# Attention and two mixture layers in fp32 on one core: two score slots per head for the first eight head pairs, and an instruction order planned with other durations

## The chip, the cores and the metric

One core of one Trainium2 chip runs the whole program. The metric is device time in microseconds of one execution, shown as the median of several runs.

## The reference

The kernel must compute, in fp32 accuracy, a thresholded attention (4 batches, 8 heads, 576 positions, 64 wide), a dense gated layer on its output (2304 tokens, 512 to 2048 to 512), and a layer of 8 experts of which each token takes one:

```python
scores = scale * q @ k.T                          # per batch and head, 576 x 576
scores = where(scores >= max(scores) - tau, scores, -1e9)
attn   = exp(scores - max(scores)); attn /= attn.sum() + 1e-9
x      = (attn @ v) -> 2304 x 512
h = x @ w_in; x = (h * sigmoid(h)) @ w_out        # the dense layer, 2048 wide
e = argmax(normalised x @ normalised expert_emb)  # one of 8 experts per token
out = gate * relu(x @ w1[e]) @ w2[e]              # 1024 wide
```

The weights of the dense layer come as fp64 and are decoded to fp32 on the chip.

## The kernel before

**The work.** Heads go in 16 pairs. A pair takes nine steps: four chunks of 128 query rows for each of its two heads (ch 0 to 3, h 0 and 1), and a ninth in which the last 64 rows of both heads stand together (ch 4). For each step TensorE (PE) writes 576 score columns to PSUM (`score_pe`, L490), VectorE (DVE) takes the row maximum (L496), ScalarE (ACT) makes the threshold (L499) and the exponential (L501), and DVE masks and sums (L516), so that P stands in SBUF. PE then transposes P (L553, L561, L569, L573), ACT or DVE copies the transposes out (L278, L280), and PE multiplies them with v (`values`, L645) in two parts per pair. The two heads of a chunk lie in the upper and lower 64 rows of the PE array and their score matmuls run side by side; in P v the two heads lie side by side in the columns. So PE works with three divisions of its array: by rows for scores, by columns for P v, whole or nearly whole for the rest. The denominators (L598 to L624) are transposed by one matmul of PE per pair (L603), go to DRAM and back, and multiply the pair's output, which then goes to DRAM.

**Filler.** The dense layer's first six of sixteen column tiles are computed inside the attention, for the blocks of 256 tokens whose batches are complete (`moe_block`, six blocks of nine): products with w_in (L685, 72 matmuls a block) and with w_out (L719, 36 a block). They have the lowest rank: PE does them when nothing of the attention can start. Decoding of the dense weights runs on DVE (L321, L326), ACT (L313, L314) and GpSimd (POOL, L331 to L335, L391) in the first part. After the attention come the rest of the dense layer (`products`, L1084, and the second product behind it) and the experts.

**PSUM.** All eight banks of 512 fp32 columns are one tile, `banks`. `BANKS` names the slots: score slots of two banks each (S0 at bank 0, S1 at 2, S2 at 6, the third only for the first `WIDE` = 40 of the 144 steps), one bank T for transposes, and M for everything else: bank 5 at first, more once the score slots that hold them are given up (`more_banks`).

**The order.** No engine chooses at run time: every engine has a fixed list, in order. `Plan` makes it while the program is built. Each `plan.task` names an engine, a duration in us that the author wrote down, the tasks it comes after, the slots (`Token`) it takes and gives, a rank, and for some a second engine that may do it instead (`alt`). `Plan.run` always starts the task that can start first by these durations, and the rank decides near ties. The semaphores are put in afterwards, by the framework, from what the instructions read and write in that order; a bank of PSUM is the unit there.

Of the kernel before, what the change touches and what calls it, by code (L numbers as in the profile page):

```python
# [9 lines left out]
F32 = mybir.dt.float32  # L10
# [15 lines left out]
    "kr": 2, "qr": 2, "vs": 2, "m": 4, "e": 2, "P": 2, "Pm": 1, "l": 2,  # L26
# [63 lines left out]
class Task:  # L90
    def __init__(self, eng, us, fn, rank, take, give, slack, more, alt):
        self.eng, self.us, self.fn, self.rank, self.take, self.give = eng, us, fn, rank, take, give
        self.slack, self.more, self.alt, self.wait, self.after, self.next, self.end = slack, more, alt, 0, [], [], None


class Plan:


    def __init__(self, bufs, banks):
# [8 lines left out]
        self.kind, self.kinds = None, defaultdict(list)  # L108

    def task(self, eng, us, fn, after=(), take=(), give=(), rank=0.0, slack=0.0, more=0.0, alt=None):  # L110

        t = Task(eng, us, fn, rank, take, give, slack, more, alt)
# [44 lines left out]
    def start(self, t, eng):  # L157
# [9 lines left out]
        return at  # L167
# [36 lines left out]
    def run(self):  # L204
        while self.n:
# [19 lines left out]
            if eng == "pe":  # L225
                us = self.clock(a, us)
            self.free[eng] = a + us
# [16 lines left out]
class Kernel:  # L244
# [44 lines left out]
    def weight_piece(self, new, src, n, name):  # L289
# [43 lines left out]
        def large():  # L333
# [7 lines left out]
            ("dve", 0.55 if wide else 0.4, dve, ["wa"], []), ("dve", 0.7 if wide else 0.55, top, [], ["wraw"]),  # L341
            ("pool", 1.26 if wide else 0.76, pool, [], ["wr"]), ("pool", 2.4 if wide else 1.5, large, [], ["wm"]),
# [39 lines left out]
    def weight_plan(self, new):  # L382
# [3 lines left out]
        def keep(o, dst):  # L386
# [6 lines left out]
            return [("act", 0.6, act, [], []), ("pool", 1.26, sub, [], ["wa"], ("dve", 0.69))]  # L393
# [85 lines left out]
    def score_pe(self, st, ch, ws, uses):  # L479

        nc = self.nc
        for h, (w, use) in enumerate(zip(ws, uses)):
            w.nm = f"{ch}{h}" + st.nm
            w.S = self.banks[:, use.slot:use.slot + 2]
        lhsT = st.o.q[:, 128 * ch:128 * ch + 128]
        for a in range(2):
            for h, w in enumerate(ws):
# [3 lines left out]
                    w.S[:, a, :288], lhsT=lhsT[rows], rhs=st.o.k[rows, 288 * a:288 * a + 288], start=True, stop=True  # L491
                )

    def score_max(self, w):
        w.m = self.apool.tile([128, 2], F32, tag="m", bufs=4, name="m" + w.nm)
        self.nc.vector.tensor_reduce(out=w.m[:, 0:1], in_=w.S[:, :, :288], axis=AX.XY, op=ALU.max, negate=True)  # L496

    def score_exp(self, w):
        self.nc.scalar.activation(out=w.m[:, 1:2], in_=w.m[:, 0:1], func=AF.Identity, bias=self.ntau, scale=-1.0)  # L499
        w.e = self.apool.tile([128, 2, 288], F32, tag="e", bufs=2, name="e" + w.nm)  # L500
        self.nc.scalar.activation(out=w.e, in_=w.S[:, :, :288], func=AF.Exp, bias=w.m[:, 0:1])  # L501

    def score_mask(self, step, w):
# [4 lines left out]
        if ch < 4:  # L508
            if h == 0:
                st.P[ch] = self.apool.tile([128, 1152], F32, tag="P", bufs=2, name=f"P{ch}" + st.nm)  # L510
# [1535 lines left out]
```

## Time and profile before

| | |
|---|---|
| median of 3 runs | 1076.0 us (1073.23 to 1076.56) |
| the profiled execution | 1079.59 us, its span 1077.8 us |
| PE busy | 983.5 us (91%) |
| DVE, ACT, POOL busy | 727.1, 529.6, 436.6 us |
| mean granted TensorE clock | 0.966 |
| denominators of pair 8 of 16 on PE | at 228.75 us |
| denominators of pair 16 | at 454.35 us |

The profile's times count from the span's start. A matmul's record lasts longer than the time until the next one may start, so a busy PE is not a PE at its peak. An fp32 matmul of L490 or L645 gives two records. "Idle ... <-" behind a row says how long the engine did nothing before it and what ended that.

### The profile page before, as it was taken

Reading aid. Unit: us, or ns where it says so; the run is one execution under the profiler, and the core shown is the slowest. Engines: PE = TensorE matmul, PEld = TensorE weight load, DVE = VectorE, ACT = ScalarE, POOL = GpSimd, SP = SyncE. Lnnn points to the kernel's source line nnn. Section 1 sums busy time; section 2 is a strip of 40 time slices with the busy share of each in tenths; the row PEclk is TensorE's granted clock in tenths of the full one; section 3 lists DMA queues with packets and bytes.
Section 4 is the critical chain, followed back from the end, with each engine's and each line's share of the span. In section 5 each row is a group of like instructions: output and inputs, shape, how many; then the busy total and the mean of one; then the engine's idle time right before and its main releaser. Section 6 shows DMA issues by size and latency. Waiting matters only on the chain. (4 is left out here: it accounts for less than half of the span.)

```text
span 1077.8 us, 18270 instructions
## 1 busy us (share of the span) xinstructions
PE 983.5 (91%) x6379; PEld 804.6 (75%) x6379; DVE 727.1 (67%) x1693; ACT 529.6 (49%) x1262; POOL 436.6 (41%) x447
## 2 busy tenths in 40 slices
PE   3878789989998999988999999999897999999995
PEld 2545466766665667667878989899886999999994
DVE  5798876767676777567768888888766534545521
ACT  4688755545464556456653333333553443454510
POOL 4997841112021012049944444444424443333210
PEclk9799989999999999999999999999997999999998
DMA  4444632222222121164423211111537554555400
GB/s 155 133 149 155 213 103 77 77 71 83 64 76 81 61 72 48 57 207 138 162 94 129 83 37 57 60 61 40 161 116 228 159 165 152 169 168 179 138 32 15
DMA packets 76398, 119.27 MB, mean 111 GB/s; under 512 B 11668, under 2 KB 38596, under 8 KB 76305
## 3 DMA queue, kind: packets, MB, share of 16 engines
q1 hardware_dynamic: 71857, 107.68, 31.4%
q0 software_dynamic: 4448, 10.40, 3.1%
q8 instruction: 51, 0.84, 0.3%
q14 instruction: 42, 0.34, 0.1%
HBM read 94.04 MB, written 24.82 MB: 110 GB/s over the span
## 5 line engine op out<-in xcount | busy, mean ns | idle before, releaser
L496 DVE TENSOR_REDUCE m<-banks 128x1 f32<-128x576 f32 x144 | 103.1, 751 | 39.0 <-PE banks L490 38.1
L516 DVE SCALAR_TENSOR_TENSOR P<-banks,m,e 128x576 f32<-128x576 f32 x128 | 103.9, 815 | 34.1 <-ACT e L501 33.8
L1065 DVE TENSOR_TENSOR wle<-rawe,whe 128x512 fp32r<-128x512 f32 x95 | 69.0, 751 | 81.5 <-ACT whe L1061 80.9
L1061 ACT ACTIVATE whe<-rawe 128x512 fp32r<-128x512 f32 x128 | 77.0, 625 | 85.7 <-PE banks L1899 29.7
L278 ACT ACTIVATE p<-banks 128x512 f32<-128x512 f32 (+2 forms) x143 | 66.6, 478 | 102.0 <-PE banks L553 83.9
L553 PE MATMUL banks<-ident,P 128*128 128x128 f32 x512 | 86.7, 294 | 32.5 <-DVE P L516 26.9
L553 PEld LDWEIGHTS banks<-ident,P 128*128 128x128 f32 x512 | 58.8, 147 | 72.9 <-DVE P L516 27.4
L501 ACT ACTIVATE e<-banks,m 128x576 f32<-128x576 f32 x144 | 105.5, 733 | 1.3 <-DVE P L516 1.2
L645 PE MATMUL banks<-p,v 128*64 128x256 f32 (+3 forms) x640 | 99.2, 438 | 6.1 <-ACT p L278 4.8
L490 PE MATMUL banks<-k,q 64*128 64x288 f32 x540 | 101.6, 448 | 1.2 <-DVE P L516 1.2
L1304 ACT ACTIVATE t<-banks 128x256 f32<-128x256 f32 x108 | 41.1, 381 | 107.5 <-PE banks L1084 105.0
L1065 POOL TENSOR_TENSOR wle<-rawe,whe 128x512 fp32r<-128x512 f32 x33 | 42.6, 1293 | 99.5 <-ACT whe L1061 77.3
L645 PEld LDWEIGHTS banks<-p,v 128*64 128x64 f32 (+1 forms) x640 | 43.1, 143 | 49.1 <-issue 20.7
L490 PEld LDWEIGHTS banks<-k,q 64*128 64x128 f32 x540 | 57.7, 195 | 23.0 <-issue 10.6
L1309 DVE SCALAR_TENSOR_TENSOR g<-t,banks 128x256 f32<-128x256 f32 x108 | 45.1, 418 | 37.0 <-ACT t L1304 33.7
L1084 PE MATMUL banks<-xs_6h,wh 128*128 128x256 f32 x216 | 61.5, 285 | 0.0
L1084 PE MATMUL banks<-xs_6h,wl 128*128 128x256 f32 x216 | 61.0, 283 | 0.0
L1084 PE MATMUL banks<-xs_6l,wh 128*128 128x256 f32 x216 | 60.9, 282 | 0.0
L710 POOL TENSOR_TENSOR gl<-g,gh 128x256 fp32r<-128x256 f32 x25 | 18.2, 731 | 103.4 <-ACT gh L704 102.2
L621 POOL TENSOR_TENSOR t<-t,rb 128x576 f32<-128x576 f32 x14 | 19.9, 1420 | 91.1 <-ACT t L278 48.6
L280 DVE COPY p<-banks 128x512 f32<-128x512 f32 (+2 forms) x81 | 43.9, 545 | 16.2 <-PE banks L553 11.8
L499 ACT ACTIVATE m<-m,ntau 128x1 f32<-128x1 f32 x144 | 41.5, 288 | 14.0 <-DVE m L496 13.6
(574 smaller groups left out, 3137.1 us busy)
## 6 DMA issues: line engine op xcount, KB each, us to landing
rawe<-moe_w SPq DMA_DIRECT2D x64, 512.0 KB, 4.5
wraw<-moe_w_in SPq DMA_DIRECT2D x12, 512.0 KB, 3.7
wraw<-moe_w_out SPq DMA_DIRECT2D x10, 512.0 KB, 3.4
q<-q SPq DMA_DIRECT2D x15, 320.0 KB, 3.9
v<-v SPq DMA_DIRECT2D x16, 288.0 KB, 3.5
x_dram<-t SPq DMA_DIRECT2D x16, 288.0 KB, 2.8
part<-po SPq DMA_DIRECT2D x18, 256.0 KB, 3.0
xc<-x_dram SPq DMA_DIRECT2D x18, 256.0 KB, 3.2
```

Of the source, the lines that this page charges most:

```text
L278: self.nc.scalar.activation(out=out, in_=src, func=AF.Copy)
L280: self.on[on].tensor_copy(out=out, in_=src)
L490: nc.tensor.matmul(w.S[:, a, :288], lhsT=lhsT[rows], rhs=st.o.k[rows, 288 * a:288 * a + 288], start=True, stop=True)
L496: self.nc.vector.tensor_reduce(out=w.m[:, 0:1], in_=w.S[:, :, :288], axis=AX.XY, op=ALU.max, negate=True)
L501: self.nc.scalar.activation(out=w.e, in_=w.S[:, :, :288], func=AF.Exp, bias=w.m[:, 0:1])
L516: self.nc.vector.scalar_tensor_tensor(out=P.rearrange("p (a x) -> p a x", a=2), in0=w.S[:, :, :288], scalar=w.m[:, 1:2], in1=w.e, op0=ALU. ...
L553: nc.tensor.transpose(T[:, 128 * j:128 * j + 128], st.P[ch][:, c:c + 128], self.ident)
L645: nc.tensor.matmul(w.av[HALF[h], :nq], lhsT=st.o.vn[rows, k, :], rhs=st.pts[part][rows, k, :], start=(j == 0), stop=(j == 4),)
L1061: self.nc.scalar.activation(out=o.tiles[0][:, 2 * a:2 * a + 2], in_=o.raw[:, 2 * a:2 * a + 2], func=AF.Copy)
L1065: self.on[on].tensor_tensor(out=o.tiles[1][:, to], in0=o.raw[:, to], in1=o.tiles[0][:, to].bitcast(F32), op=ALU.subtract)
L1084: self.nc.tensor.matmul(h[:, :n], lhsT=lhs(a, kk), rhs=z[:, kk, :], start=(kk == 0 and i == 0), stop=(kk == 3 and i == 2))
L1309: nc.vector.scalar_tensor_tensor(out=o.g, in0=o.t, scalar=1.0, in1=self.banks[:, use.slot, :BLK], op0=ALU.add, op1=ALU.mult)
```

## The change

- **Score slots.** For the first 72 steps (eight pairs, before: 40 steps) each head has two slots of its own: A0 and A1 for h 0 in banks 0 to 2, B0 and B1 for h 1 in banks 3 to 5. A slot is 688 columns and holds the 576 scores as four pieces of 144 columns, 172 apart, so that no piece crosses a bank. Slot 0 lies in the first bank and in the first 148 columns of the second; slot 1 in the rest of the second and in the third. A score step pair is now 16 records of 144 columns there, where it was 8 of 288; after step 72 it is as before, with one slot per head. The exponentials have three buffers, before two.
- **M.** T is bank 6, M bank 7 alone until the last wide mask; then banks 2 and 5 come to M.
- **P v.** The five matmul pairs of a part are one task; they were five tasks.
- **Planner.** Each change between scores, P v and the rest costs 0.1 us in the plan (`SWITCH`), and many written durations are others.

The core of the diff:

```diff
-    "kr": 2, "qr": 2, "vs": 2, "m": 4, "e": 2, "P": 2, "Pm": 1, "l": 2,
+    "kr": 2, "qr": 2, "vs": 2, "m": 4, "e": 3, "P": 2, "Pm": 1, "l": 2,
-BANKS = {"S0": [0], "S1": [2], "S2": [6], "T": [4], "M": [5, 6, 7, 0, 1, 2, 3, 4]}
-WIDE = 40
+BANKS = {"A0": [0], "A1": [1], "B0": [0], "B1": [1], "T": [6], "M": [7, 2, 5, 0, 1, 3, 4, 6]}
+WIDE = 72
+PIECE, APART = 144, 172
+SWITCH = 0.1
...
-        return at
+        return at + SWITCH if eng == "pe" and t.mode != self.mode else at
...
-            w.S = self.banks[:, use.slot:use.slot + 2]
+            bank = 3 if use.tag[0] == "B" else 0
+            if use.wide:
+                at = 512 * bank + 4 * APART * use.slot
+                w.S = self.flat[:, at:at + 4 * APART].rearrange("p (a x) -> p a x", x=APART)[:, :, :PIECE]
+            else:
+                w.S = self.banks[:, bank:bank + 2, :288]
...
-                    w.S[:, a, :288], lhsT=lhsT[rows], rhs=st.o.k[rows, 288 * a:288 * a + 288], start=True, stop=True
+                    w.S[:, a], lhsT=lhsT[rows], rhs=st.o.k[rows, c * a:c * a + c], start=True, stop=True
...
-        self.more_banks = {bank: Token("gate") for bank in (0, 2, 4, 6)}
+        self.more_banks = {x: Token("gate") for x in ("wide", "narrow", "T")}
...
-                    turn = int(s + i) % (3 if s < WIDE else 2)
-                    w.use = Token(f"S{turn}")
+                    w.use = Token(f"{'AB'[i]}{(9 * n // 2 + n % 2 + (a + 1) // 2) % 2 if s < WIDE else 0}")
+                    w.use.wide = s < WIDE
...
-                    "pe", 0.97, partial(self.score_pe, st, ch, pe, [w.use for w in pe]), o.there + self.last_s,
+                    "pe", 1.18, partial(self.score_pe, st, ch, pe, [w.use for w in pe]),
+                    o.there + self.last_s + ([] if s < WIDE else self.last_wide),
...
-                "dve", 0.73, partial(self.score_mask, step, w), [t] + list(masks.values())[-1:],
+                "dve", 0.81, partial(self.score_mask, step, w), [t] + list(masks.values())[-1:],
...
-                for i, fn in enumerate(mms):
-                    t = plan.task(
-                        "pe", us, fn, (t,) if t else moved[part] + o.v_there + av[-1:],
+                t = plan.task(
+                    "pe", 5 * us, partial(run_all, mms), moved[part] + o.v_there + av[-1:],
+                    (tok,) if part else (tok, t_use), (part_use[part], o.v_use), rank=s + 1, mode="values",
+                )
```

What this does to the order, at three places. In the changed kernel L503 are the scores (L490 before), L567 and L575 transposes (L553, L561), L583 and L587 those of the last rows (L569, L573), L617 the denominators (L603), L659 P v (L645), L699 and L733 the dense layer's two products (L685, L719), L509 the maximum (L496), L530 the mask (L516), L515 the exponential (L501).

First, PE in the fourth pair (k_559 before, k_532 now): scores, transposes, P v and the denominators of the pair before it. Before:

```order
L490 MATMUL banks<-k_559,q_554 128x288 x4
L553 MATMUL banks<-ident,P_781 128x128 x4
L569 MATMUL banks<-ident,Pm 128x64 x4
L573 MATMUL banks<-ident,Pm 64x64
L569 MATMUL banks<-ident,Pm 128x64 x4
L573 MATMUL banks<-ident,Pm 128x64
L490 MATMUL banks<-k_559,q_554 128x288 x4
L603 MATMUL banks<-ident,l_629 9x128
L553 MATMUL banks<-ident,P_859 128x128 x4
L645 MATMUL banks<-p_763,v_452 64x320 x10
L553 MATMUL banks<-ident,P_859 128x128 x4
```

and now:

```order
L503 MATMUL banks<-k_532,q_513 128x144 x8
L567 MATMUL banks<-ident,P_779 128x128 x4
L617 MATMUL banks<-ident,l_645 9x128
L503 MATMUL banks<-k_532,q_513 128x144 x8
L583 MATMUL banks<-ident,Pm 128x64 x4
L587 MATMUL banks<-ident,Pm 64x64
L583 MATMUL banks<-ident,Pm 128x64 x4
L587 MATMUL banks<-ident,Pm 128x64
L567 MATMUL banks<-ident,P_891 128x128 x4
L659 MATMUL banks<-p_798,v_442 64x320 x10
L567 MATMUL banks<-ident,P_891 128x128 x4
```

The second chunk's scores moved ahead of the transposes of the last rows of the pair before, since a second slot of each head is there for them.

Second, what such instructions wait for, a little further in the same pair. DVE before (maxima of the third chunk of the third pair, both heads, a copy, and their masks):

```order
L496 TENSOR_REDUCE m2002_717<-banks_99 128x1 [waits PE_49]
L496 TENSOR_REDUCE m2102_722<-banks_99 128x1 [waits PE_49]
L280 COPY p002_675<-banks_99 128x256 [waits PE_49,Activation_49]
L516 SCALAR_TENSOR_TENSOR P202_737,l02_629<-banks_99,m2002_717,e2002_725 128x576 [waits Activation_49]
L516 SCALAR_TENSOR_TENSOR P202_737,l02_629<-banks_99,m2102_722,e2102_735 128x576 [waits Activation_49]
```

and DVE now (first two chunks of the fourth pair; the digits of a name are chunk, head, batch, pair):

```order
L509 TENSOR_REDUCE m0003_853<-banks_99 128x1
L509 TENSOR_REDUCE m0103_865<-banks_99 128x1 [waits PE_49]
L328 TENSOR_SCALAR wa140_873<-wraw140_715 128x512 [waits DMAHW1_49,Pool_49]
L509 TENSOR_REDUCE m1003_880<-banks_99 128x1 [waits PE_49,Activation_49]
L530 SCALAR_TENSOR_TENSOR P003_891,l03_890<-banks_99,m0003_853,e0003_870 128x576
L333 SCALAR_TENSOR_TENSOR wa140_873<-wraw140_715,wa140_873 128x512 [waits DVE_49]
L530 SCALAR_TENSOR_TENSOR P003_891,l03_890<-banks_99,m0103_865,e0103_883 128x576 [waits Activation_49]
```

The maximum of the second chunk (m1003) now waits for ACT too, that is, for the exponential of the first chunk of the same head, whose slot shares a bank with its own. PE has the like: of the scores of the third chunk the last two matmuls, the pieces in the shared banks, wait for DVE and ACT:

```order
L503 MATMUL banks_99<-k03_532,q03_513 128x144 x6
L503 MATMUL banks_99<-k03_532,q03_513 128x144 [waits DVE_49]
L503 MATMUL banks_99<-k03_532,q03_513 128x144 [waits Activation_49]
L567 MATMUL banks_99<-ident_60,P103_927 128x128 [waits Activation_49]
L567 MATMUL banks_99<-ident_60,P103_927 128x128 x3
```

Before, the scores at that place waited for one thing only, the mask of the step whose slot they take, and no maximum waited for ACT.

Third, PE at the start of the thirteenth pair (k_3037 before, k_2901 now). Before:

```order
L490 MATMUL banks<-k_3037,q_3025 128x288 x4
L645 MATMUL banks<-p_3223,v_2811 64x320 x10
L553 MATMUL banks<-ident,P_3338 128x128 x4
L490 MATMUL banks<-k_3037,q_3025 128x288 x4
L553 MATMUL banks<-ident,P_3338 128x128 x4
L553 MATMUL banks<-ident,P_3376 128x128 x4
L561 MATMUL banks<-ident,P_3338 128x128
L561 MATMUL banks<-ident,P_3376 128x128
L490 MATMUL banks<-k_3037,q_3025 128x288 x4
```

and now:

```order
L503 MATMUL banks<-k_2901,q_2891 128x288 x4
L617 MATMUL banks<-ident,l_2998 9x128
L733 MATMUL banks<-who_110,gh_5_3125 128x512
L733 MATMUL banks<-who_110,gl_5_3131 128x512
L733 MATMUL banks<-wlo_111,gh_5_3125 128x512 x2
L699 MATMUL banks<-xh_3101,whi_100 128x256
L699 MATMUL banks<-xl_3102,whi_100 128x256
L699 MATMUL banks<-xh_3101,wli_101 128x256
```

Before, there was no filler in the first half of this pair; now filler stands there, because the filler as a whole moved to later pairs.

## Rows read from the trace of the kernel before

**Rows 1.** The page, busy tenths of the span in 40 slices, PE and DVE.

```profile
PE   3878789989998999988999999999897999999995
DVE  5798876767676777567768888888766534545521
```

**Rows 2.** Windows, all engines: stretch and length, busy (instructions) per engine, PEclk, DMA.

```profile
0.00:229.00 229.00, 184.52 (x1164) 119.18 (x1165) 177.50 (x346) 146.67 (x336) 129.85 (x106) 0.93 0.40 128
229.00:454.00 225.00, 210.85 (x1427) 148.27 (x1427) 155.66 (x321) 122.03 (x301) 34.87 (x38) 0.98 0.22 70
45.00:131.00 86.00, 72.79 (x456) 42.15 (x455) 76.84 (x144) 67.83 (x151) 72.91 (x56) 0.93 0.53 172
```

**Rows 3.** Timeline of PE: the denominators of pairs 8 and 16.

```profile
228.75 0.28 PE L603 MATMUL banks<-ident,l 128*9 128x128 f32 x1
454.35 0.28 PE L603 MATMUL banks<-ident,l 128*9 128x128 f32 x1
```

**Rows 4.** Groups of instructions by line, 0 to 229 us, DVE and ACT.

```profile
L496 DVE TENSOR_REDUCE m<-banks 128x1 f32<-128x576 f32 x73 | 52.3, 750 | 12.9 <-PE banks L490 12.1
L516 DVE SCALAR_TENSOR_TENSOR P<-banks,m,e 128x576 f32<-128x576 f32 x64 | 51.7, 812 | 15.5 <-ACT e L501 15.3
L280 DVE COPY p<-banks 128x512 f32<-128x512 f32 (+2 forms) x33 | 17.3, 529 | 5.1 <-PE banks L553 2.9 <-ACT p L278 1.2 <-PE banks L573 0.5
L698 DVE SCALAR_TENSOR_TENSOR g<-t,banks 128x256 f32<-128x256 f32 x12 | 4.7, 416 | 0.6 <-ACT t L692 0.5
L710 DVE TENSOR_TENSOR gl<-g,gh 128x256 fp32r<-128x256 f32 x6 | 4.7, 778 | 0.5 <-ACT gh L704 0.4
L391 DVE TENSOR_TENSOR wlo<-wa,who 128x512 fp32r<-128x512 f32 x2 | 2.2, 1120 | 2.4 <-ACT who L388 2.4
L621 DVE TENSOR_TENSOR t<-t,rb 128x576 f32<-128x576 f32 x1 | 1.1, 1148 | 0.0
L501 ACT ACTIVATE e<-banks,m 128x576 f32<-128x576 f32 x72 | 52.6, 731 | 1.2 <-DVE P L516 1.2
L499 ACT ACTIVATE m<-m,ntau 128x1 f32<-128x1 f32 x72 | 20.7, 288 | 8.6 <-DVE m L496 8.3
```

**Rows 5.** The first pair's scores, by source line.

```profile
L490 PE MATMUL banks<-kfirst,qfirst x36: 402/507/846, 6.1 to 35.5; 64*128 64x288 f32 x32, 128*128 128x288 f32 x4
```

**Rows 6.** Timeline: scores of two heads, P v of a part, and transposes behind one.

```profile
78.18 1.24 PE L490 MATMUL banks<-k,q 64*128 64x288 f32 x8
84.40 2.53 PE L645 MATMUL banks<-p,v 128*64 128x256 f32 x20
86.86 0.20 PEld L553 LDWEIGHTS banks<-ident,P 128*128 128x128 f32 x2 [0.39 <-ACT e L501]
```

**Rows 7.** Timeline: a run of maxima on DVE and an exponential on ACT.

```profile
62.02 2.08 DVE L496 TENSOR_REDUCE m<-banks 128x1 f32<-128x576 f32 x3 [0.58 <-PE banks L490]
63.48 0.73 ACT L501 ACTIVATE e<-banks,m 128x576 f32<-128x576 f32 x1
```

**Rows 8.** Windows of L685 alone, then of L719 alone: PE busy, PEld busy, PEclk, DMA.

```profile
240.00:280.00 40.00, 9.27 (x72) 8.67 (x72) 1.00 0.22 69
240.00:280.00 40.00, 6.79 (x24) 4.13 (x24) 1.00 0.22 69
```

**Rows 9.** Windows, all engines, pairs 10 to 13.

```profile
280.00:320.00 40.00, 38.58 (x278) 27.94 (x278) 27.10 (x59) 23.33 (x59) 7.14 (x8) 1.00 0.24 74
320.00:360.00 40.00, 34.33 (x204) 21.54 (x201) 26.12 (x50) 17.43 (x41) 4.83 (x4) 0.91 0.25 80
```

**Rows 10.** Timeline: the last P v, and a wait of PE behind it.

```profile
454.90 5.17 PE L645 MATMUL banks<-p,v 128*64 128x320 f32 x20 [0.27 <-DVE p L280]
462.41 0.38 PE L1084 MATMUL banks<-xs7h,whi 128*128 128x256 f32 x1 [1.10 <-ACT xs7h L1231]
```

**Rows 11.** Windows after the attention, all engines, and a group of the page.

```profile
500.00:520.00 20.00, 17.97 (x104) 15.54 (x103) 15.56 (x29) 11.50 (x32) 19.41 (x25) 0.91 0.38 119
L1065 POOL TENSOR_TENSOR wle<-rawe,whe 128x512 fp32r<-128x512 f32 x33 | 42.6, 1293 | 99.5 <-ACT whe L1061 77.3
```

More of the change, by code (lines that the diff above doesn't have):

```diff
@@ L108, in __init__, with task @@
         self.kind, self.kinds = None, defaultdict(list)
-    def task(self, eng, us, fn, after=(), take=(), give=(), rank=0.0, slack=0.0, more=0.0, alt=None):
-        t = Task(eng, us, fn, rank, take, give, slack, more, alt)
+        self.mode = ""
+    def task(self, eng, us, fn, after=(), take=(), give=(), rank=0.0, slack=0.0, more=0.0, alt=None, mode=""):
+        t = Task(eng, us, fn, rank, take, give, slack, more, alt, mode)
         for tok in give:
@@ L226, in run @@
                 us = self.clock(a, us)
+                self.mode = t.mode
             self.free[eng] = a + us
@@ L886, in attend @@
             mask = masks[ch, h] = plan.task(
-                "dve", 0.73, partial(self.score_mask, step, w), [t] + list(masks.values())[-1:],
-                ((p_use[ch],) if h == 0 else ()) + ((l_use,) if a == 0 else ()), use + [self.more_banks[scores.bank]], rank=s - 2, slack=0.1,
-            )
+                "dve", 0.81, partial(self.score_mask, step, w), [t] + list(masks.values())[-1:],
+                ((p_use[ch],) if h == 0 else ()) + ((l_use,) if a == 0 else ()), use + [self.more_banks[x] for x in ("wide", "narrow")[s >= WIDE:]], rank=s - 2,
+                slack=0.1,
+            )
+            if s < WIDE:
+                self.last_wide = [mask]
             part = min(ch // 2, 1)
@@ L894, in attend @@
                 tok = Token(tag)
-                give = [self.more_banks[4]] if tag == "T" else []
+                give = [self.more_banks["T"]] if tag == "T" else []
                 if i and ch < 4:
-                    after, us, used = [masks[x, y] for x in (ch - 1, ch) for y in range(2)], 0.215, [p_use[ch - 1], p_use[ch]]
+                    after, us, used = [masks[x, y] for x in (ch - 1, ch) for y in range(2)], 0.24, [p_use[ch - 1], p_use[ch]]
                 else:
-                    after, us, used = [mask], 0.43 if ch < 4 else 0.27, [p_use[ch]]
-                t = plan.task("pe", us, partial(turn, tok), after, (tok,), used, rank=s + -0.5, slack=0.1)
+                    after, us, used = [mask], 0.46 if ch < 4 else 0.3, [p_use[ch]]
+                t = plan.task("pe", us, partial(turn, tok), after + (begun[part:part + 1] if i else []), (tok,), used, rank=s + -0.5, slack=0.1)
                 for cols, move in pieces:
@@ L934, in attend @@
         t = plan.task("sp", 0.45, store, (t,), (), (tok[1],), rank=s, more=2.2)
-        t = [plan.task("sp", 0.6, partial(load, i), (t,), (tok[2],) if i == 0 else (), rank=s, more=2.4) for i in range(3)]
-        t = plan.task("pool", 1.36, mul, t + moved["x"], (), (tok[2],), rank=s, alt=("dve", 0.66))
+        t = [plan.task("sp", 1.8, partial(run_all, [partial(load, i) for i in range(3)]), (t,), (tok[2],), rank=s, more=2.4)]
+        t = plan.task("pool", 1.36, mul, t + moved["x"], (), (tok[2],), rank=s, alt=("dve", 0.95))
         x_there.append(plan.task("sp", 0.45, out, (t,), (), (t_use,), rank=s, more=2.4))
```

45 lines of the change are left out of this document (22 added, 23 removed).

## The prediction

> **What bounds the kernel now.** I read the busy slices first, then windows, then the groups of each engine. The attention fills the first 454 us [rows 3] and falls into two halves of eight pairs that are limited by different things. In the first half DVE is the fullest engine: 177.5 of 229 us, and 76.84 of 86 us, 89%, in the stretch from 45 to 131 us, where there is no filler yet and the weights are decoded; PE has 72.79 of 86 there [rows 2]. The slices show the same change of roles: DVE's digits fall from 7 and 8 to 6 and 7 while PE's rise to 9 [rows 1]. DVE's own idle time has two main causes: 15.3 us for an exponential of ACT, 12.1 us for scores of PE [rows 4]. Both are what too few score slots look like: the next scores are late, or DVE has nothing but the mask of the step just handed to ACT. In the second half PE is the bound: 210.85 of 225 us [rows 2]. After the attention PE is nearly full too, so what the attention gains is gained at the end, unless decoding gets in the way (below).
>
> **The change, part by part.** Six terms. Counts of instructions come from the order of both kernels, durations from the rows.
>
> *1. The first eight pairs.* They end at 228.75 us [rows 3]. What DVE has to do in them becomes less, because filler leaves and copies go to ACT: 19 copies fewer at 0.529 us (-10.1), 3 subtractions of L391 at 1.12 (-3.4), 6 of L710 at 0.778 (-4.7), 7 gates of L698 at 0.416 (-2.9), 2 products of L621 more at 1.148 (+2.3) [rows 4]: 177.5 - 18.8 = 159 us. ACT gets 14 copies and loses filler, about even at 147, so it stays below DVE. At DVE's share of 0.893 in the stretch without filler [rows 2], 159 us need 178 us, plus the 6 us before the first scores [rows 5]: 184 us. That is the better end. Against it stand the new waits on the shared banks. The order has 12 maxima that now wait for an exponential of ACT (none before) and 15 exponentials that wait for a mask of DVE (2 before). The trace of before never shows such a wait, it shows the opposite: an exponential of 0.73 us from 63.48 lies wholly within a run of maxima on DVE [rows 7]. So its price lies between nothing, where the other engine is through anyway, and a whole exponential, 0.731 us. I take it whole for 27 of them, 20 us, because DVE and ACT keep strict order and what is behind the waiting instruction waits too: 204 us. There are further new waits, of masks and exponentials for scores of PE, which the worse end takes in: 219 us. Term: **-25 us**, ends -45 and -10.
>
> Scores in twice as many pieces cost PE between nothing (the same columns) and as much again, 1.24 us [rows 6], for each of 32 two-head groups: 0 to 40 us of PE time. PE does not pay it on the path while DVE sets the pace: 184.5 us busy less some 24 of filler that leaves, plus a third of 40, is 174 of 204 us. If that cover were gone, the 14 us would count.
>
> *2. Filler that comes later.* By the denominators of pair 8, before has 144 products of L685 and 47 of L719 behind it, the change 60 and none. In a filled window 72 of L685 hold PE for 9.27 us, 0.129 each, and 24 of L719 for 6.79, 0.283 each [rows 8]. So 84 x 0.129 + 47 x 0.283 = **+24 us** for the second half, which PE bounds. By the records' start to start it would be some 20; that is the other end.
>
> *3. A hole that closes.* From 320 to 360 us PE is busy 34.33 us, against 38.58 in the window before, and its mean granted clock is 0.91, part of it at 1.2 GHz: a loss of 4.2 and 3.6 us [rows 9]. That is the thirteenth pair, in which the filler of the finished batches is used up and that of the next is not there yet. In the new order every one of the last eight pairs has filler. **-6 us** of 7.8, ends -8 and 0.
>
> *4. Fewer changes of the array's division.* From pair 9 on there are 104 changes between scores, P v and the rest, against 118; loading stops up to 0.39 us at one [rows 6]. 14 x 0.18 = **-2.5 us**, ends -1 and -5.5. P v in one piece holds a transpose back by up to its 2.53 us [rows 6]; the copies behind it then come later, but PE goes on with filler, so I cost that at nothing.
>
> *5. The seam to the tail.* The last P v runs at half clock, 5.17 us, and PE then waits 1.10 us for the last denominators' product [rows 10]. Now 28 filler products of L719 stand between, so PE has work there. They are in term 2. **-2 us**, ends 0 and -3.
>
> *6. After the attention.* POOL is full, 19.41 of 20 us, while it decodes the last weights [rows 11], and the plan gives it 5 more subtractions of L1065 of 1.293 us and 3 smaller ones. Most are behind PE's 18 early tiles. **+1 us**, ends 0 and +5.
>
> Sum: -25 + 24 - 6 - 2.5 - 2 + 1 = -10.5 us. The profiled execution took 1079.6 us (span 1077.8 and 1.8 around it) and would take 1069.1. The median of the runs shown is 3.6 lower; from 1076.0 the forecast is **1065.5 us**.
>
> **The rivals.**
> *A. Sharing a bank undoes the second slot (slower).* Mechanism: slots 0 and 1 of a head meet in bank 1 (or 4), every access there by another engine is put in order, and the scores of the chunk after next wait in the middle of their group for the exponential of the last chunk, with the transposes queued behind them on PE. For it: the rows with the new waits in the order. Against: the chain by itself, scores 0.4, maxima of both heads 2 x 0.75, threshold 0.288, exponential 0.731 [rows 4] and some 0.4 between engines, is 3.3 us a chunk or 15 us a pair, below the 20 us of work that DVE has per pair. If stalls bring the first half to 222 us, the gain there is 7 and the sum -7 + 24 - 10.5 + 1 = +8: 1084 us. It decides from about 214 us at the eighth denominators; above that the later filler costs more than the slots bring.
> A rule stands behind it: the Trainium skill, "PSUM — Partial Sum Buffer", section "PSUM bank collisions raise a hardware error", says that two engines must not be at one bank on the same partitions at once, even at different addresses, and asks for semaphores by bank. By that rule the new waits cannot be left out; the trace of before bears it out only so far that its overlapping accesses go to slots in different banks.
> *B. DVE keeps its 89% in spite of the waits.* The first half takes 184 us, the rest as above: 1046 us. For it: 9 of 10 waits may be met already, since the plan starts the waiting instruction late anyway. Against: in the plan these waits do not exist.
> *C. The second half pays the filler dearer.* Pairs 9 to 16 have no second slot; with more filler between, masks wait longer for transposes and the chain of one slot per head stretches. Another 2 us a pair beyond term 2 is +8, so about 1074: no change. For it: DVE waits there for PE at the maxima already. Against: PE waits hardly at all in that half.
> That the plan does not come out as planned at all (the changes cancel) is in A and C.
>
> **How the numbers follow.** About 3 us, 0.3%, is what a measurement can tell from no change. My forecast, first half between 196 and 211 us: 0.50, with its own range 1055 to 1074. A: 0.22. B: 0.16. C: 0.12. Faster by over 0.3% (below 1072.8): nearly all of the forecast, 0.46, B, and 0.02 of C: 0.64. Within: 0.04 of the forecast, 0.07 of C and 0.03 of A: 0.14. Slower (above 1079.2): 0.22. The ends of all terms together reach from 1035 to 1096; leaving a tenth at each side, of B below and of A above, gives 1050 to 1083.
>
> **What would show it.** The denominators of pair 8 near 204 us and those of pair 16 near 437 (228.75 and 454.35 before; 28 filler products now come behind the latter); DVE over 80% busy until 204 us, its idle time before L496 for PE near nothing, and new idle time before maxima that ends at ACT; the last eight pairs at 29 us each (28.2 before), with no pair whose PE busy falls below 37 of 40 us; the stretch behind the attention as long as before. Wrong if the eighth denominators come after 214 us (A), if from the eighth to the sixteenth denominators it takes over 239 us (C), or if time is lost while POOL decodes after the attention.

## The result and the profile after

The changed kernel takes **1065.6 us** (median of 16 runs) against 1078.7 us of the kernel before (16 runs beside it): ratio **0.9874**, 95% interval [0.985, 0.9898]. Two of the 16 runs of the changed kernel fell into a slower state; the median counts them, the ratio does not. The prediction was 1065.5 us from a median of 1076.0, a ratio of 0.990. The profiled execution has a span of 1064.0 us, against 1077.8.

The page of the changed kernel, the two rows of [rows 1] and TensorE's granted clock:

```profile
PE   5877778999999999987999999999896999999995
DVE  5868888667777677477678787888565545445521
...
PEclk8978999999999999998999999999898999999998
```

PE's 9s begin at the eighth slice and now hold without a break until the end of the attention (slice 17), where before there were 8s and a half-clock stretch. The stages, cut at the denominators of pairs 4, 8 and 16 on PE (L617 now), in the changed kernel; columns as in [rows 2]:

```profile
209.34 0.27 PE L617 MATMUL banks<-ident,l 128*9 128x128 f32 x1
...
435.96 0.28 PE L617 MATMUL banks<-ident,l 128*9 128x128 f32 x1
```

```profile
0.00:116.60 116.60, 84.46 (x627) 60.39 (x627) 86.12 (x161) 81.35 (x178) 75.32 (x62) 0.85 0.42 139
116.60:209.30 92.70, 75.56 (x658) 54.40 (x656) 72.75 (x150) 64.27 (x149) 48.60 (x39) 1.00 0.39 130
209.30:436.00 226.70, 223.23 (x1577) 162.81 (x1575) 161.12 (x336) 130.84 (x326) 42.14 (x49) 1.00 0.22 72
436.00:1064.00 628.00, 591.73 (x3812) 541.60 (x3812) 386.79 (x1025) 260.94 (x625) 279.65 (x307) 0.97 0.38 119
```

The same stages of the kernel before:

```profile
0.00:116.70 116.70, 85.59 (x487) 49.87 (x487) 93.44 (x175) 83.28 (x182) 88.08 (x71) 0.90 0.48 154
116.70:228.70 112.00, 98.68 (x676) 69.06 (x675) 83.78 (x171) 63.40 (x155) 41.77 (x35) 0.95 0.32 102
228.70:454.30 225.60, 211.41 (x1433) 148.81 (x1433) 156.11 (x321) 122.03 (x301) 34.87 (x38) 0.98 0.22 70
454.30:1077.80 623.50, 587.83 (x3786) 536.82 (x3784) 393.76 (x1027) 260.88 (x625) 271.89 (x303) 0.97 0.38 119
```

Against the denominators of [rows 3], the first four pairs take the same time as before, pairs 5 to 8 take 19.3 us less, pairs 9 to 16 take 1.1 us more, and the stretch behind them 4.5 us more. The third rows say what happened in pairs 9 to 16: PE was idle for 225.60 - 211.41 = 14.2 us of them before and is for 226.70 - 223.23 = 3.5 us now, while it is busy 11.8 us longer.

For all kernels below I split a stage's time in two. **Lost** is PE's idle time, plus half of its busy time in stretches where the granted clock was 1.2 GHz instead of 2.4. The rest is PE's **work** at full clock. This is an estimate: it counts each busy microsecond at the lower level as half a microsecond of work. In the first four pairs, where no kernel has filler, work comes out between 67.2 and 77.0 us, so a few us of work in one stage say little. Before: 956.0 us of work and 121.8 lost; after: 950.9 and 113.1.

### The profile page after: what moved, and what is told of

Same layout as the page of the kernel before. It is cut to its first block, busy times and chain, and to the rows that moved or that the text cites. A ratio compares the mean times of both kernels' runs of the same rounds, so it can differ in the third digit from the quotient of the medians.

```text
span 1064.0 us, 18940 instructions
## 1 busy us (share of the span) xinstructions
PE 975.0 (92%) x6667; PEld 819.2 (77%) x6667; DVE 706.8 (66%) x1670; ACT 537.4 (51%) x1277; POOL 445.7 (42%) x455
## 4 chain that ended last, share of the span: by engine, by line
PE 70%; issue 8%; DVE 6%; ACT 5%; DMA 4%; POOL 4%; SPq 1%; another core or an unknown queue 0%; POOLq 0%; DVEq 0%; ACTq 0%
PE banks L1099 21%; PE banks L1351 12%; PE banks L503 7%; PE banks L659 7%; PE banks L1914 6%; PE banks L567 5%; PE banks L733 4%; PE banks L699 4%; ACT e L515 2%; PE banks L1910 2%; DVE m L509 2%; DVE P L530 1%; ACT p L285 1%; DMA xb<-x_dram 1%; PE banks L1851 1%
## 5 line engine op out<-in xcount | busy, mean ns | idle before, releaser
L509 DVE TENSOR_REDUCE m<-banks 128x1 f32<-128x576 f32 x144 | 104.5, 751 | 36.6 <-PE banks L503 33.4
L530 DVE SCALAR_TENSOR_TENSOR P<-banks,m,e 128x576 f32<-128x576 f32 x128 | 103.7, 815 | 33.4 <-ACT e L515 19.6
L1080 DVE TENSOR_TENSOR wle<-rawe,whe 128x512 fp32r<-128x512 f32 x92 | 64.5, 724 | 79.5 <-ACT whe L1076 76.2
L515 ACT ACTIVATE e<-banks,m 128x576 f32<-128x576 f32 x144 | 105.6, 734 | 12.9 <-PE banks L503 9.1
L503 PE MATMUL banks<-k,q 64*128 64x144 f32 (+3 forms) x792 | 98.7, 352 | 12.2 <-DVE m L509 7.3
L285 ACT ACTIVATE p<-banks 128x512 f32<-128x512 f32 (+2 forms) x161 | 75.1, 483 | 63.1 <-PE banks L567 47.8
L567 PE MATMUL banks<-ident,P 128*128 128x128 f32 x512 | 85.8, 292 | 22.9 <-ACT p L285 14.5
L567 PEld LDWEIGHTS banks<-ident,P 128*128 128x128 f32 x512 | 58.5, 146 | 52.9 <-ACT p L285 20.5
L659 PE MATMUL banks<-p,v 128*64 128x256 f32 (+3 forms) x640 | 92.4, 426 | 0.0
L503 PEld LDWEIGHTS banks<-k,q 64*128 64x128 f32 (+1 forms) x792 | 70.7, 195 | 25.5 <-DVE m L509 8.9
L1080 POOL TENSOR_TENSOR wle<-rawe,whe 128x512 fp32r<-128x512 f32 x36 | 46.8, 1301 | 91.6 <-ACT whe L1076 70.9
L1324 DVE SCALAR_TENSOR_TENSOR g<-t,banks 128x256 f32<-128x256 f32 x108 | 45.2, 419 | 47.2 <-ACT t L1319 35.7
L659 PEld LDWEIGHTS banks<-p,v 128*64 128x64 f32 (+1 forms) x640 | 41.2, 139 | 42.9 <-issue 22.8
L1937 POOL DMA_INDIRECT out<-yr,idx x25 | 25.5, 1020 | 52.1 <-DVE yr L1949 39.5
L699 PE MATMUL banks<-xh,whi 128*128 128x256 f32 x144 | 43.9, 305 | 3.5 <-ACT p L285 1.6
```

What stands on the lines that cost most here:

```text
L285: self.nc.scalar.activation(out=out, in_=src, func=AF.Copy)
L503: nc.tensor.matmul(w.S[:, a], lhsT=lhsT[rows], rhs=st.o.k[rows, c * a:c * a + c], start=True, stop=True)
L509: self.nc.vector.tensor_reduce(out=w.m[:, 0:1], in_=w.S, axis=AX.XY, op=ALU.max, negate=True)
L515: self.nc.scalar.activation(out=w.e, in_=w.S, func=AF.Exp, bias=w.m[:, 0:1])
L530: self.nc.vector.scalar_tensor_tensor(out=P.rearrange("p (a x) -> p a x", a=w.S.shape[1]), in0=w.S, scalar=w.m[:, 1:2], in1=w.e, op0=ALU.i ...
L567: nc.tensor.transpose(T[:, 128 * j:128 * j + 128], st.P[ch][:, c:c + 128], self.ident)
```

## The experiments

Twelve kernels, in three groups. All times are us; "lost" is by pairs and then behind the attention. The span and what is right of it come from one profiled execution of each kernel, the ratio from all its runs; executions of one kernel differ (those of the changed one from 1058.2 to 1071.9 us in the runs that the ratio counts), and the profiled ones of e_pv5 and e_noswitch were some 4 us above their medians. The expectations call the products with w_in (L685, now L699) G and those with w_out (L719, now L733) H; they are the filler.

| kernel | ratio, 95% interval | pair 8 at | pair 16 at | span | lost 1-4 | 5-8 | 9-16 | behind | work |
|---|---|---|---|---|---|---|---|---|---|
| before | 1 | 228.7 | 454.3 | 1077.8 | 41.7 | 17.1 | 17.6 | 45.4 | 956.0 |
| after | 0.9874 [0.985, 0.9898] | 209.3 | 436.0 | 1064.0 | 46.8 | 17.1 | 3.5 | 45.7 | 950.9 |
| e_slots | 0.9972 [0.9952, 0.9993] | 203.6 | 429.9 | 1070.4 | 44.9 | 18.0 | 9.9 | 43.3 | 954.2 |
| e_plan | 1.0513 [1.0479, 1.0547] | 269.6 | 512.9 | 1137.9 | 78.9 | 18.9 | 39.0 | 48.4 | 952.7 |
| e_three72 | 1.0137 [1.0114, 1.0159] | 243.0 | 470.2 | 1091.2 | 76.5 | 16.1 | 3.6 | 42.4 | 952.6 |
| e_b72 | 1.0041 [1.0019, 1.0064] | 201.6 | 431.0 | 1080.7 | 40.6 | 11.9 | 13.9 | 53.7 | 960.6 |
| e_pv5 | 1.0041 [1.0013, 1.0069] | 214.5 | 446.4 | 1082.9 | 42.8 | 24.4 | 7.5 | 54.4 | 953.9 |
| e_noswitch | 1.0005 [0.9981, 1.0029] | 212.8 | 437.6 | 1080.1 | 46.8 | 21.7 | 7.5 | 52.7 | 951.5 |
| e_wide36 | 1.0189 [1.014, 1.0237] | 234.0 | 472.0 | 1091.8 | 38.7 | 19.8 | 33.9 | 41.4 | 958.0 |
| e_jit | 0.9927 [0.9891, 0.9962] | 217.2 | 443.9 | 1067.9 | 46.2 | 27.5 | 4.7 | 37.6 | 952.0 |
| e_three72_pv5 | 1.0235 [1.0197, 1.0273] | 250.3 | 480.1 | 1108.0 | 82.9 | 16.2 | 4.8 | 50.9 | 953.2 |
| e_oldus | 0.9917 [0.9894, 0.994] | 214.6 | 440.6 | 1068.5 | 38.5 | 22.4 | 0.6 | 45.2 | 961.8 |
| e_jit2 | 0.9953 [0.9927, 0.9978] | 216.5 | 446.8 | 1072.3 | 47.6 | 25.8 | 3.6 | 42.8 | 952.5 |
| e_wide108 | 1.0296 [1.0251, 1.0341] | 211.3 | 458.7 | 1110.6 | 42.6 | 23.8 | 39.8 | 50.2 | 954.1 |

### Slots or planner: four kernels

**e_slots**: the kernel before with the slot layout of the change and nothing of its planner.

```diff
-WIDE = 40
+WIDE = 72
+PIECE, APART = 144, 172
...
+                    w.use = Token(f"{'AB'[i]}{(9 * n // 2 + n % 2 + (a + 1) // 2) % 2 if s < WIDE else 0}")
```

> The kernel before with the new slot layout alone (two slots per head for eight pairs in shared banks, pieces of 144, three buffers for exponentials); old durations in the planner, no price of a tiling change, P v as five tasks. Theory T1 (the second slot is what helps, and the planner's other durations are worth a few us): eighth denominators at 200 to 212 us as in the changed kernel (209.3), ratio to the kernel before 0.985 to 0.992. Rival T2 (what helps is that filler leaves the first half, whatever the slots are): the same here, since this order has only 36 products of G and none of H before the eighth denominators against 144 and 47; it is told from T1 by the run with three old slots for eight pairs. Rival T3 (the new durations and P v in one piece do it): eighth denominators may be early, but the end is not: ratio 0.997 to 1.01.

Measured: 0.9972, at the edge of T3's range (from 0.997) and outside T1's (to 0.992). The eighth denominators came at 203.6 us, as T1 and T2 had it.

**e_plan**: the changed kernel with the old slots. Its planner holds two more edits than the list of the change names: the second transposes of a step come after the first copy of their part, and the three loads of the denominators are one task. They are in all kernels that start from the changed one. The two old buffers for exponentials, instead of three, come back here with the old slots.

```diff
-BANKS = {"A0": [0], "A1": [1], "B0": [0], "B1": [1], "T": [6], "M": [7, 2, 5, 0, 1, 3, 4, 6]}
-WIDE = 72
...
+BANKS = {"S0": [0], "S1": [2], "S2": [6], "T": [4], "M": [5, 6, 7, 0, 1, 2, 3, 4]}
+WIDE = 40
...
```

> The changed kernel with the old score slots (three single ones for 40 steps, then two), and the new durations, the price of a tiling change and P v in one piece. T1 and T2: eighth denominators at 224 to 230 us, because the first half keeps all its filler (144 products of G, 72 of H); ratio 0.995 to 1.0, from fewer tiling changes and the fuller second half. T3: ratio 0.985 to 0.990.

Measured: 1.0513. Every theory missed: the new planner on the old slots makes the span 60 us longer. Half of it is in the first four pairs (148.5 us, before 116.7), ahead of any filler. There PE's transposes wait longer for masks of DVE. The waits of PE from 40 to 160 us in this kernel (engine, line, what it waited for, us in total, times, longest):

```profile
PE banks L558 <- DVE P L521: 25.2, 9, 5.1
```

and in the kernel before:

```profile
PE banks L553 <- DVE P L516: 8.4, 4, 4.3
```

**e_three72**: e_plan with `WIDE` 72, so that the three single slots stay for eight pairs.

```diff
-WIDE = 40
+WIDE = 72
```

> As the run with the new planner and the old slots, but the three single slots stay for eight pairs instead of 40 steps (WIDE 72): no two slots share a bank, a head has one and a half slots, and the filler leaves the first half (72 products of G, none of H there, against 60 and none in the changed kernel). T1: the missing half slot costs 10 us or more in the first half: eighth denominators at 215 to 225 us, ratio 0.995 to 1.0. T2: eighth denominators at 205 to 213 us, ratio 0.983 to 0.990, as the changed kernel, and better than it if the shared banks cost something.

Measured: 1.0137, eighth denominators at 243.0 us; slower than either theory had it. The first four pairs lose 76.5 us, nearly as much as in e_plan (78.9), but pairs 9 to 16 lose 3.6 us instead of 39.0. Those pairs in e_plan:

```profile
269.60:512.90 243.30, 221.80 (x1419) 153.51 (x1417) 159.70 (x330) 121.66 (x298) 31.00 (x36) 0.92 0.19 63
```

and in e_three72:

```profile
243.00:470.20 227.20, 223.61 (x1559) 163.41 (x1558) 159.39 (x335) 129.09 (x319) 37.90 (x43) 1.00 0.21 70
```

Between these two kernels only the step at which the third slot goes differs, and it is worth 42 us by the medians.

**e_b72**: the kernel before with that one number changed.

```diff
-WIDE = 40
+WIDE = 72
```

> The kernel before with one number changed: WIDE 72 for 40, so the three single slots stay for eight pairs and the filler leaves the first half (36 products of G there, none of H). T1: ratio 1.0 to 1.01, the filler comes later and nothing pays for it. T2: eighth denominators at 203 to 213 us, ratio 0.985 to 0.992. T3: ratio 1.0 or above.

Its stages:

```profile
0.00:117.70 117.70, 87.17 (x488) 50.39 (x489) 92.27 (x175) 82.77 (x182) 88.00 (x71) 0.91 0.46 153
117.70:201.60 83.90, 73.60 (x501) 45.30 (x500) 68.19 (x138) 59.28 (x138) 38.52 (x30) 0.98 0.38 122
201.60:431.00 229.40, 218.96 (x1494) 156.09 (x1492) 157.91 (x329) 123.96 (x311) 38.41 (x42) 0.99 0.21 68
431.00:1080.70 649.70, 606.29 (x3903) 553.22 (x3901) 393.43 (x1035) 268.61 (x644) 281.30 (x310) 0.97 0.36 116
```

Measured: 1.0041, as T1 and T3 had it; T2 missed. Without a second slot, the eighth denominators come 27.1 us earlier than before, more than with the whole change. What left the first half is 108 products of G and 47 of H: 108 x 0.129 + 47 x 0.283 = 27.2 us by [rows 8]. By the split above, pairs 5 to 8 have 22.9 us less work for PE and 5.2 less lost. And the end is not earlier: the filler comes later, 9 us of G and 11 of H only behind the attention, and that stretch loses 8.3 us more than before. So an early eighth pair is worth nothing by itself, as term 2 of the prediction had it. With the same 36 products in the first half, e_slots loses 62.9 us in the first eight pairs and e_b72 52.5: the two shared slots per head did not make the first half faster than three separate ones (203.6 and 201.6 us).

### What carries the gain: four kernels

The first group suggested T4, that the gain sits in pairs 9 to 16.

**e_pv5**: the changed kernel, P v as five tasks.

```diff
-                    "pe", 5 * us, partial(run_all, mms), moved[part] + o.v_there + av[-1:],
...
+                for i, fn in enumerate(mms):
+                    t = plan.task(
+                        "pe", us, fn, (t,) if t else moved[part] + o.v_there + av[-1:],
```

> The changed kernel with P v again as five tasks (still priced as a tiling change). Theory T4, formed after the first four runs: the time is PE's work at full clock (956.0 us before, 950.9 after) plus what PE loses in idle time and half clock (121.8 and 113.1); the gain sits in pairs 9 to 16, where the loss falls from 17.6 to 3.5 us because filler is there in every pair, and in 5 us less PE work from P v in one piece. T4 expects here: work 953 to 956 us, loss in pairs 9 to 16 below 7 us, ratio 0.989 to 0.993. Rival T3b (P v in one piece is what makes the planner's order good or bad): loss in pairs 9 to 16 back at 10 to 18 us, ratio 0.995 to 1.005. If P v in one piece only costs (it did nothing for the old slots): ratio below 0.986.

Measured: 1.0041, which only T3b's range holds. The work is T4's (953.9), the loss of 7.5 us in pairs 9 to 16 lies between the two. Most of the 16 us more that are lost lie elsewhere, 7.3 in pairs 5 to 8 and 8.7 behind the attention, where neither theory expected anything. Pairs 9 to 16 have the same filler in both kernels, seven changes of the array's division more than in the changed kernel, and 224.5 us of work against 223.1, which would be 0.2 us a change. That is no clean price: e_jit2 below has the same filler there, by its trace five changes fewer than the changed kernel, and 226.7 us of work.

**e_noswitch**: the changed kernel with no price on such a change.

```diff
-SWITCH = 0.1
+SWITCH = 0.0
```

> The changed kernel with the planner's price for a tiling change at 0 instead of 0.1. T4: more changes of tiling, PE work 1 to 4 us above 950.9, loss in pairs 9 to 16 still below 7 us, ratio 0.988 to 0.992. Rival T3c (the price of a change is what groups the work): work above 954, ratio 0.994 or more.

Measured: 1.0005; work 951.5, lost 7.5 in pairs 9 to 16. The ratio is T3c's, its mechanism is not: the work hardly rose. 7.0 us more are lost behind the attention, 4.6 in pairs 5 to 8, 4.0 in pairs 9 to 16. In this kernel and in e_pv5 most of the gain of pairs 9 to 16 is there, and the total gain is not.

**e_wide36**: the changed kernel with the two shared slots for four pairs.

```diff
-WIDE = 72
+WIDE = 36
```

> The changed kernel with two shared slots per head for four pairs instead of eight (WIDE 36): the banks come free earlier and pairs 5 to 8 take 144 products of G and 72 of H again, against 60 and none. T4: the filler of the last batches is used up early again, the loss in pairs 9 to 16 is 14 us or more, ratio 0.996 to 1.005. T1 (the second slot in the early pairs is what helps): four of eight pairs keep it, so half the gain, ratio 0.992 to 0.995, and the loss in pairs 9 to 16 stays below 7.

Measured: 1.0189, lost 33.9 us in pairs 9 to 16: T4 has the mechanism and the loss (14 or more), but put the ratio too low, and T1 is refuted here. Pairs 12 and 16 have 4 and 7 products of H left and nothing else, and the pair behind the first of them is slow as well. Its stages:

```profile
110.70:234.00 123.30, 109.75 (x711) 75.35 (x710) 93.69 (x181) 69.13 (x165) 51.42 (x43) 0.94 0.35 112
234.00:472.00 238.00, 215.63 (x1412) 150.36 (x1411) 161.50 (x332) 122.48 (x299) 26.57 (x32) 0.95 0.20 64
...
340.00:360.00 20.00, 15.28 (x86) 8.94 (x84) 12.00 (x27) 7.85 (x19) 0.00 (x0) 0.83 0.13 46
```

PE is idle for 22.4 us of the second row, against 3.5 in the changed kernel, and in the last row, where filler has run out, it works 15.28 of 20 us at a mean clock of 0.83.

**e_jit**: a control, one planned duration moved by 0.01 us.

```diff
-                "dve", 0.81, partial(self.score_mask, step, w), [t] + list(masks.values())[-1:],
+                "dve", 0.82, partial(self.score_mask, step, w), [t] + list(masks.values())[-1:],
```

> A control: the changed kernel with one planned duration 0.82 for 0.81 us (the mask's), which changes nothing in the work, only the order by chance. If the order's quality is stable under such changes: ratio 0.985 to 0.990. If it is a matter of chance to the size of the effect: outside that.

Measured: 0.9927, outside the stable range. The loss in pairs 9 to 16 stayed (4.7 us); pairs 5 to 8 lost 10.4 more, the stretch behind the attention 8.1 less.

### Checks on the rest: four kernels

**e_three72_pv5**: e_three72 with P v as five tasks; the edit is that of e_pv5.

> The run with three old slots for eight pairs and the new planner (ratio 1.0137, loss of PE in the first four pairs 76.5 us against 46.8 with the shared slots), now with P v as five tasks again. Theory T5 (with single slots the next scores stand behind transposes and a whole P v, and PE idles until it runs at half clock; the second slot hides that): loss in the first four pairs falls to 40 to 52 us, ratio 0.99 to 1.003. Rival T6 (P v has no part in it; the new durations put transposes right ahead of the scores of a single slot): loss stays above 65 us, ratio 1.005 to 1.02.

Measured: 1.0235, 82.9 us lost in the first four pairs. T5 is refuted: P v in one piece is not what spoils the single slots. The loss is T6's, the ratio a little above its range. But T6 names the durations, and no run shows that: the price of a change and the second transposes' place behind the first copy are in this kernel too, and none of the three was taken out on single slots.

**e_oldus**: the changed kernel with the old durations.

```diff
-                    "pe", 1.18, partial(self.score_pe, st, ch, pe, [w.use for w in pe]),
+                    "pe", 0.97, partial(self.score_pe, st, ch, pe, [w.use for w in pe]),
...
-                "dve", 0.81, partial(self.score_mask, step, w), [t] + list(masks.values())[-1:],
+                "dve", 0.73, partial(self.score_mask, step, w), [t] + list(masks.values())[-1:],
```

> The changed kernel with the old durations in the planner; the price of a tiling change, P v in one piece and the slots stay. T4 (filler in every one of pairs 9 to 16: the smallest count is 45 here, 44 in the changed kernel): loss in pairs 9 to 16 below 8 us, ratio 0.985 to 0.993. Rival T3d (the durations bring the gain): ratio 0.997 or more.

Measured: 0.9917, lost 0.6 us in pairs 9 to 16: T4. Once the slots are there, the gain doesn't need the new durations. Its total loss of 106.7 us is the smallest of all; its work, 961.8, the largest.

**e_jit2**: a second control.

```diff
-                    "pe", 1.18, partial(self.score_pe, st, ch, pe, [w.use for w in pe]),
+                    "pe", 1.17, partial(self.score_pe, st, ch, pe, [w.use for w in pe]),
```

> A second control: the changed kernel with the planned time of a score group 1.17 for 1.18 us; filler per pair is nearly the same. Order stable: ratio 0.985 to 0.990. Otherwise it adds to the spread that the first control showed (0.9927).

Measured: 0.9953; lost 3.6 us in pairs 9 to 16, 25.8 in pairs 5 to 8. So three orders of one change give 0.9874, 0.9927 and 0.9953: all faster than before, and 0.8% apart, two to three times what one measurement is uncertain by. That of the changed kernel is the best of the three. The same spread lies on e_pv5 and e_noswitch, which are one order each: e_noswitch is only 0.5% above e_jit2, so whether the price of a change carries the gain stays open. No such control was made of the kernel before, which is one order too, so part of the 0.5 to 1.3% may be its draw.

**e_wide108**: the changed kernel with the shared slots for twelve pairs.

```diff
-WIDE = 72
+WIDE = 108
```

> The changed kernel with two shared slots for twelve pairs instead of eight (WIDE 108). Pairs 9 to 12 then have 12, 36, 24 and 78 filler products instead of 44, 84, 52 and 80. T4: a pair with little filler loses about 4 us, as pairs 5 to 8 do (17.1 in four), so the loss in pairs 9 to 16 is 12 to 20 us, ratio 0.995 to 1.008. T1 (the second slot itself saves PE's idle time): loss there below 6 us, ratio 0.975 to 0.987.

Measured: 1.0296, 39.8 us lost in pairs 9 to 16. T1 is refuted outright: more steps with a second slot cost 45 us by the medians. T4 missed as well, with 12 to 20 us of loss and 0.995 to 1.008. Pairs 9 to 11, with 12, 36 and 24 products, lose 18.4 us, 6 each where T4 said 4. Pair 12, where the slots change, is a thing of its own that no theory had: it takes 58.9 us and loses 15.0. From 287 to 302 us PE does 48 products of w_in in a row with no scores between, at the lower clock:

```profile
290.00:310.00 20.00, 15.08 (x73) 10.79 (x72) 5.40 (x12) 5.13 (x13) 1.61 (x2) 0.59 0.10 29
```

No experiment beats the changed kernel.

### What all kernels show together

Leave out e_wide108, whose pairs 9 to 12 have other slots: pairs 9 to 16 of before, after and the eleven others are 104 pairs with one slot per head. I put each pair's filler at 0.129 us a product of G and 0.283 of H [rows 8]:

| filler in the pair | pairs | mean lost per pair | most |
|---|---|---|---|
| over 9 us | 88 | 0.7 us | 3.4 us |
| 7.4 to 8.9 us | 7 | 2.1 us | 4.6 us |
| 6.2 us (48 of G alone) | 5 | 7.2 us | 8.8 us |
| 1 to 2 us | 4 | 10.1 us | 12.4 us |

A pair of the attention leaves PE some 10 us that only filler can take, and much of what is missing of it is lost. This compares orders and is no experiment: pairs with 6.2 us of filler lose 7.2, more than the 3.8 that they lack, so when the filler comes within a pair must count as well. That is what the eight pairs with the larger slots do for the time: while six banks belong to scores, M has one bank, the filler can't run ahead, and it is there when each of the later pairs wants it. In the plan of the changed kernel the smallest of these pairs has 44 products, 10.6 us.

The same kernels show that planner and slots need each other. In pairs 9 to 16 it counts how long scores hold six banks: the old planner loses 17.6 us there with 40 steps, 13.9 and 9.9 with 72; the new one 39.0 and 33.9 with 40 and 36 steps, and 0.6 to 7.5 with 72, on single slots (3.6 in e_three72) as on shared ones. In the first four pairs the kind of slot counts: there the new planner loses 76.5 to 82.9 us on single slots and 38.5 to 47.6 on shared ones, the old planner 40.6 to 44.9 on either. (The third buffer for exponentials goes with the shared slots in all of them, so the two are not told apart.)

## Why the prediction was right, and where it was not

**The total** was right within the bound, and the case that came is the forecast, with the first half at 209.3 us inside its 196 to 211. By stages the prediction had -25 for the first half, +7.6 for pairs 9 to 16 (terms 2 to 4 less the 28 products that come behind, 7.9 us) and +6.9 behind the attention (the 7.9, terms 5 and 6). Measured: -19.4, +1.1 and +4.5. The sum of -10.5 became -13.8: the errors of the first two stages, +5.6 and -6.5, nearly cancel. That the median is met to 0.1 us is luck. The prediction started from 1076.0 us, where 16 runs gave 1078.7, and took off 10.5, where 13.1 came; and the two controls, the same change with one planned duration moved by 0.01 us, took 1070.0 and 1073.5 us.

**Term 1 failed in its reason.** It said that DVE sets the pace of the first half, that less work for DVE at a share of 89% makes it shorter, and that 27 new waits on shared banks cost 20 us. It called DVE the fullest engine of the first half, but [rows 2] have PE at 184.52 us there and DVE at 177.5; DVE is the fuller one only from 45 to 131 us. DVE's work did come down as forecast, to 86.12 + 72.75 = 158.9 us against 159. Its share in the stretch without filler fell to 59.48 of 75 us, 79%, and in pairs 5 to 8 it is 72.75 of 92.7, 78%. (The sign "over 80% until 204 us" did not fit the forecast's own 159 of 204, 78%.)

```profile
45.00:120.00 75.00, 56.54 (x427) 39.38 (x423) 59.48 (x106) 53.84 (x123) 54.36 (x41) 0.84 0.41 135
```

Groups of DVE and ACT in the changed kernel, 0 to 209.3 us, against [rows 4]:

```profile
L509 DVE TENSOR_REDUCE m<-banks 128x1 f32<-128x576 f32 x72 | 53.0, 749 | 16.0 <-PE banks L503 12.9 <-issue 1.6 <-ACT e L515 1.3
L515 ACT ACTIVATE e<-banks,m 128x576 f32<-128x576 f32 x72 | 52.9, 735 | 12.9 <-PE banks L503 9.1 <-DVE P L530 2.3 <-DVE m L509 1.1
L530 DVE SCALAR_TENSOR_TENSOR P<-banks,m,e 128x576 f32<-128x576 f32 x64 | 51.5, 812 | 18.6 <-PE banks L503 10.9 <-ACT e L515 4.9 <-ACT wm L321 1.8
```

The waits that I priced at 20 us, maxima for an exponential and exponentials for a mask, are 1.3 and 2.3 us. Those that I had put into the worse end only, masks and exponentials held up by scores of PE, are 10.9 and 9.1, and the maxima still wait 12.9 us for scores where I had said near nothing. Together these five are 36.5 us, where the same five were 13.3 before: 23 us more, near the 20, with the wrong engines in it. Against that, masks wait for their exponential 4.9 us where it was 15.3, and waits of two engines overlap, so the 23 us are no length of time. (The reading behind the 20 us was a little off, too: the exponential of [rows 7] ends at 64.21 us, 0.11 behind the run of maxima.) By the rule of the Trainium skill ("PSUM — Partial Sum Buffer", section "PSUM bank collisions raise a hardware error"), two engines must not be at one bank and the same partitions at once. The trace agrees so far as sharing goes with waits of a new kind: of the 15.5 us before masks in [rows 4], 15.3 ended at the exponential, and now 10.9 of 18.6 end at scores of PE.

What shortened the first half is filler that left it, second slot or not: e_b72 shows that. It is 19.3 us of PE's work in pairs 5 to 8 (94.9 to 75.6), with the loss unchanged at 17.1. The filler took DVE's time as well (83.78 to 72.75 us there), so that PE's part is what counted is argued: before, PE was idle for 13.3 us of those pairs and DVE for 28.2. The second slot itself buys something else, which I had not seen: with the new planner, single slots lose 76.5 us in the first four pairs and shared ones 46.8.

**Term 2** (+24) was nearer to its other end, some 20. PE's work rose by 15.1 us in pairs 9 to 16 and by 4.3 behind them, 19.4 together; up to 2.5 of the difference may be term 4's.

**Term 3 was mis-sized**: -6 us for one hole in the thirteenth pair, where the loss in pairs 9 to 16 fell by 14.1. Pair 13 had 5.9 of the 17.6 us; the other seven had 11.7, in pieces of up to 3.2 us that [rows 9] don't show as such: the window from 320 to 360 us holds 22 us of pair 12 (3.2 us lost) and 18 of pair 13. As predicted, none of the stretches of 40 us from 200 to 440 us falls below 37 busy us any more (the least is 38.27).

**Term 4** took 14 changes fewer at 0.18 us, a price drawn from a stop of 0.39 us that ends, by its row in [rows 6], at an exponential of ACT and so need not be a change's. By the traces pairs 9 to 16 have only 4 to 8 fewer, by where one starts to count, so the term is -0.7 to -1.4 us at its own price, and no run measures that price (e_pv5 and e_jit2 point apart). **Score pieces** cost PE nothing, as assumed. A two-head group of twice as many pieces takes 1.25 us, against 1.24 [rows 6], and 1.25 is the median of all such groups that run in one go:

```profile
125.52 1.25 PE L503 MATMUL banks<-k,q 64*128 64x144 f32 x16
```

**Terms 5 and 6**: less the 7.9 us of filler, the stretch behind the attention got 3.4 us shorter where -1 was expected. The last P v has its clock back, 3.06 us against 5.17, and the wait of 1.10 us [rows 10] is now 0.65:

```profile
442.59 3.06 PE L659 MATMUL banks<-p,v 128*64 128x320 f32 x20
...
447.56 0.38 PE L1099 MATMUL banks<-xs7h,whi 128*128 128x256 f32 x1 [0.65 <-ACT xs7h L1246]
```

**The rivals.** A put its turning point at 214 us for the eighth denominators. The controls had them at 217.2 and 216.5 and were faster than before, since their pairs 9 to 16 took 226.7 and 230.3 us, where terms 2 to 4 came to 233.2. B and C did not come: the first half took 209.3 us and not 184, with DVE busy for 76% of it, and pairs 9 to 16 took 226.7 us, not 239.

**What stays open**: what in the new planner ruins the first four pairs on single slots (durations, the price of a change, or the second transposes' new place), and why the stretch behind the attention loses between 37.6 and 54.4 us; with one profile a kernel, order and execution can't be told apart there. The shared banks were not tried against separate ones in one and the same order, and no second order of the kernel before was measured.

## What to carry to other kernels

Where low-rank filler shares an engine with a chain, ask first in which stretch it runs out: moving it is neutral where the engine stays busy, and worth the engine's gaps where it would have run dry. Find that by the filler per unit of the chain, not by one window with a visible hole. An order from a planner is one draw: move a written duration by 1% and measure again before a gain under 1% is put down to an edit.

## What was not expected

- A change of one number (`WIDE`, 40 to 72) moved 27 us out of the first half and nothing out of the total; setting it to 36 in the changed kernel cost 29 us by the medians.
- Two parts of a change that are near nothing or harmful alone, the slots (0.9972) and the planner on the old slots (1.0513), gave 0.9874 together.
- The granted clock of PE stayed at 2.4 GHz from 110 to 488 us in the changed kernel, with the engine busy for 223.23 of 226.70 us in pairs 9 to 16; in e_three72 and e_plan, where it idled for 52 and 54 us in the first four pairs, it was 0.80 of full speed there on average.
